# Retention state kept as 64 x 64 blocks instead of zero-padded 128 x 128 blocks, with heads m and m + 4 paired

## The chip, the cores and the metric

One core of one Trainium2 chip runs the whole program. The metric is the device time of one execution in microseconds (us), median of several runs.

## The reference

Three stages follow one another. Stage one is retention (attention with a decay and no softmax) for 4 sequences, 8 heads, 576 positions, 64 wide:

```python
scores = scale * np.matmul(q, k.transpose(0, 1, 3, 2))
gamma = 1.0 - 2.0 ** (-5.0 - np.arange(H))
Dmat = np.where(rel >= 0, gamma[:, None, None] ** rel, 0.0)    # rel = i - j
x = np.matmul(scores * Dmat, v)                                # -> 2304 tokens x 512
```

Stage two sends every token to one of 8 experts (argmax of x @ w_gate), runs relu(x @ w1) @ w2 there and multiplies by the gate. Stage three is a dense layer with a softmax-weighted activation and a layer norm. The change is in stage one.

## The kernel before, in words

**Retention by chunks.** Each of the 4 sequences is cut into 4 chunks of 128 positions and a last one of 64, so there are 20 chunks; c is a chunk's place in its sequence (0 to 4). For a chunk, the output x is the sum of two products. The *value products* (L437) multiply the decayed scores P inside the chunk with v. The *state products* (L432, only for c > 0) multiply the decayed queries qd with the state S that earlier chunks of the sequence left. After the chunk, S is updated: 8 products kd x v go to PSUM (o_D, L446) and VectorE adds them to S (o_Sadd, L456 and L458); the last chunk of a sequence needs no update.

**Tiles of the TensorE array.** All of this is float32, and each float32 matmul leaves two records (two passes) in the trace. The page writes the part of the array that a matmul uses as rows*columns: 128*64 is half the columns, 64*128 half the rows, 64*64 a quarter. Two heads share the 128 partitions of qT, kT and qd. In S the two heads of a pair stand on the diagonal of a 128 x 128 block, and the rest of the block is zeros that are set once. So a state product contracts over all 128 rows, gives both heads of a pair at once (128 columns out), and uses 128*64: 64 positions at a time, 8 matmuls for a full chunk. Value products use 128*64 as well, 16 matmuls of 64 columns. The scores (o_S, L417) use row halves, one head of a pair on each.

**The order of work.** The order on every engine is written by hand. PERIOD lists the steps of one period; ('PV', 2) means that period i runs the step for chunk i - 2. DRAIN writes out what follows period 19. Around the change it reads, in a period: T (transposes of k and q, age 0), S (age 1), D (age 2), Sq (age 3, ScalarE: sum of squares of x; bs on VectorE and pw, a power on GpSimd, make a factor of it), ..., R and L (routing, ages 6 and 5), PV (age 2), X (age 4, transposes of normalised rows), hi (age 3, ScalarE: x times its factor to half precision), Sadd (age 2), xr (age 4, ScalarE), lo (age 3, VectorE: the rest of x). So Sq, hi and lo read x of chunk i - 3 in the period in which PV writes x of chunk i - 2. x has two buffers, each one PSUM bank (psX, bufs=2). In DRAIN, hi:17 stands behind PV:18, hi:18 ahead of PV:19, and lo:18 behind PV:19.

**Loads.** SyncE issues every load in one in-order queue (load, L354). Each k and each v of a chunk is one DMA (L368), each q of two chunks one DMA (L365). Loads of chunk i + 3 are issued in period i, once their buffers are free (k has 4, v 6, q 4).

**What comes behind.** DRAIN scatters the routed rows to memory, loads the first 192 rows of expert 0 back (L540) and runs them (ehm, L256 to L258). The experts and stage three follow, each in one fixed order.

Of the kernel before, what the change touches and what calls it, by code (L numbers as in the profile page):

```python
# [10 lines left out]
F32 = mybir.dt.float32  # L11
# [10 lines left out]
DM = H * D  # L22
E = 8
F = 1024
CH = 128
# [30 lines left out]
def host_constants():  # L56

    gam = 1.0 - 2.0 ** (-5.0 - np.arange(H, dtype=np.float64))
    p = np.arange(128)
    slot = 2 * (np.arange(H) % 4) + np.arange(H) // 4  # L60
    i_j = (p[None, :] - p[:, None])[:, None, :].astype(np.float64)
    decay = np.where(i_j >= 0, gam[slot][None, :, None] ** np.maximum(i_j, 0.0), 0.0) * (XS / np.sqrt(float(D)))
    pair = gam[2 * np.arange(4)[None, :] + (p // 64)[:, None]]
    qdec = pair[:, :, None] ** (CH + p)[None, None, :].astype(np.float64) * (XS / np.sqrt(float(D)))
    kdec = gam[None, None, :] ** -(np.arange(CPB)[None, :, None] * CH + p[:, None, None]).astype(np.float64)
    f = {}
    f["ident"] = np.eye(128)
    f["gch"] = pair ** float(CH)
    f["kdec"] = kdec.reshape(128, -1)
    f["iota8"] = np.tile(np.arange(E), (128, 1))  # L70
    f["ebase"] = np.tile(np.arange(E) * NR, (128, 1))
    f["tri8"] = np.tile((np.arange(E)[None, :] < np.arange(E)[:, None]).astype(np.float32).reshape(1, -1), (128, 1))
    f["cols"] = np.tile([COLS[0] - EARLY] + list(COLS[1:]), (128, 1))
    f["first"] = np.tile([100.0 * E * NR] + [float(E - e) for e in range(1, E)], (128, 1))
    f["nrows"] = np.tile([rows16(c) for c in COLS], (128, 1))

    un = p[:, None] + 128 * np.arange(NUT)[None, :]
    f["unit"] = np.concatenate([un % NUNIT, p[:, None] % (UNIT - 1)], axis=1)
    f["uexp"] = 1 + np.concatenate([un // NUNIT, p[:, None] // (UNIT - 1)], axis=1)
    f["iblk"] = np.tile(np.arange(NBLK), (128, 1))  # L80
    f["nhalf"] = np.tile([-0.5, 0.5], (128, 1))
    cols, parts, at = {}, [], 0
    for k, a in f.items():
        cols[k] = (at, at + a.shape[1])
        at += a.shape[1]
        parts.append(a.astype(np.float32))
    c32 = np.ascontiguousarray(np.concatenate(parts, axis=1), dtype=np.float32)
    h = {}
    h["ident16"] = np.eye(128)
    h["tris"] = (p[:, None] < p[None, :]).astype(np.float32)  # L90
    h["ones"] = np.ones((128, 128))
    h["iota128"] = np.tile(p, (128, 1))

    h["ida"], h["idb"] = np.zeros((128, NCH)), np.zeros((128, NCH))
    for ch in range(NCH):
        b, c = divmod(ch, CPB)
        n = min(CH, S - c * CH)
        h["ida"][:n, ch], h["idb"][:n, ch] = np.divmod(b * S + c * CH + np.arange(n) - NOID, 64)
    h["ida"] *= 64
    h["acc0"] = np.tile(np.arange(E) * (NR // 128), (128, 1))  # L100
    cols16, parts, at = {}, [], 0
    for k, a in h.items():
        cols16[k] = (at, at + a.shape[1])
        at += a.shape[1]
        parts.append(a.astype(np.float16))
    c16 = np.ascontiguousarray(np.concatenate(parts, axis=1), dtype=np.float16)
    tok = np.zeros((1, 1), dtype=np.int32)
    return (c32, cols, c16, cols16, tok, np.ascontiguousarray(decay.reshape(128, -1), dtype=np.float32),
            np.ascontiguousarray(qdec, dtype=np.float32))
# [3 lines left out]
def tile_attention_moe_solu(ctx: ExitStack, tc: tile.TileContext, a: dict, cols, cols16):  # L113
# [216 lines left out]


    at_stack = ExitStack()
    psX = at_stack.enter_context(tc.tile_pool(name="psX", bufs=2, space=PSUM))
    ap_ = at_stack.enter_context(tc.tile_pool(name="attn", bufs=2))
    at_one = at_stack.enter_context(tc.tile_pool(name="at_one", bufs=1))
    st = [dict() for _ in range(NCH + 1)]
    decay = at_one.tile([128, H, 128], F32, name="decay")
    qdec = at_one.tile([128, CPB - 1, 4, 128], F32, name="qdec")

    states = [at_one.tile([128, 4, 128], F32, name=f"S{i}") for i in range(2)]  # L340
    misc = psB.tile([128, 512], F32, tag="b1", name="misc")
    sps = misc[:, 0:4 * D].rearrange("p (m d) -> p m d", d=D)
    lgp = misc[:, 4 * D:4 * D + 2 * E].rearrange("p (t e) -> p t e", e=E)
# [7 lines left out]
    def heads(t, n):  # L351
        return t[:n].rearrange("p (h d) -> p h d", h=H)

    def load(ch, names="qkv"):  # L354

        b, c = divmod(ch, CPB)
        n = csize(ch)
        for nm in names:
            if nm == "q":
                if c % 2:  # L360
                    st[ch]["q"] = st[ch - 1]["q"]
                    continue
                n2 = min(2 * CH, S - c * CH)
                t = ap_.tile([128, H, 2, D], F32, tag="q", bufs=4, name="q")
                sp.dma_start(t[:n2 // 2], a["q"][b, :, c * CH:c * CH + n2, :].rearrange("h (p r) d -> p h r d", r=2))  # L365
            else:
                t = ap_.tile([128, DM], F32, tag=nm, bufs={"k": 4, "v": 6}[nm], name=nm)
                sp.dma_start(heads(t, n), a[nm][b, :, c * CH:c * CH + n, :].rearrange("h p d -> p h d"))  # L368
            st[ch][nm] = t

    def o_T(ch, n, s):
# [14 lines left out]
    def q_half(ch, n, s, o):  # L386

        for r in range(2):
            yield (s["qT"][64 * o:64 * o + 64, :, :n].rearrange("p m (j r) -> p m r j", r=2)[:, :, r],
                   s["qp"][64 * r:64 * r + 64, o::2, :n // 2])  # L390

    def o_qe(ch, n, s):
        s["qT"] = ap_.tile([128, 4, 128], F32, tag="qT", name="qT")
# [29 lines left out]

    def o_PV(ch, n, s):
        b, c = divmod(ch, CPB)
        xo = s["x"] = psX.tile([128, DM], F32, tag="b0", name="xo")

        halves = [slice(i, i + 64) for i in range(0, n, 64)]
        if c:
            for m in range(4):  # L430
                for i in halves:
                    pe.matmul(xo[i, m * 128:(m + 1) * 128], lhsT=s["qd"][:, m, i], rhs=states[b % 2][:, m, :],  # L432
                              start=(m == 0), stop=False)
        for h in range(H):
            d = slice(h * D, (h + 1) * D)
            for i in halves:
                pe.matmul(xo[i, d], lhsT=s["P"][:n, 4 * (h % 2) + h // 2, i], rhs=s["v"][:n, d],  # L437
                          start=(c == 0 and h == 0), stop=(h == H - 1))

    def o_D(ch, n, s):  # L440
        if ch % CPB == CPB - 1:
            return
        for m in range(4):
            for r in range(2):
                h = 2 * m + r
                pe.matmul(sps[64 * r:64 * r + 64, m, :], lhsT=s["kd"][:n, h * D:(h + 1) * D], rhs=s["v"][:n, h * D:(h + 1) * D],  # L446
                          start=(m == 0), stop=(m == 3))

    def o_Sadd(ch, n, s):
        b, c = divmod(ch, CPB)  # L450
        if c == CPB - 1:
            return
        for r in range(2):
            d = states[b % 2][64 * r:64 * r + 64, :, 64 * r:64 * r + 64]
            if c == 0:
                dve.tensor_copy(d, sps[64 * r:64 * r + 64])  # L456
            else:
                dve.tensor_tensor(d, d, sps[64 * r:64 * r + 64], op=ALU.add)  # L458

    def o_Sq(ch, n, s):  # L460
        junk = ap_.tile([128, DM], F16, tag="junk", name="junk")
        s["ss"] = ap_.tile([128, 1], F32, tag="ss", name="ss")
        act.activation(junk[:n], s["x"][:n], AF.Square, accum_out=s["ss"][:n])

    def o_bs(ch, n, s):
        s["base"] = ap_.tile([128, 1], F32, tag="base", name="base")
# [4 lines left out]

    def o_hi(ch, n, s):
        s["row"] = ap_.tile([128, 2 * DM], F16, tag="row", bufs=9, name="row")
        act.activation(s["row"][:n, 0:DM], s["x"][:n], AF.Copy, scale=pwall[:n, ch, 0:1])

    def o_lo(ch, n, s):
        dve.scalar_tensor_tensor(s["row"][:n, DM:2 * DM], s["x"][:n], pwall[:n, ch, 0:1], s["row"][:n, 0:DM],
                                 op0=ALU.mult, op1=ALU.subtract)

    def o_X(ch, n, s):  # L480
# [153 lines left out]
    def warm(n):  # L634

        if n:
            ps = psX.tile([128, DM], F32, tag="b0", name="wps")
            for _ in range(n):
                pe.matmul(ps, lhsT=zero[:, 0:128], rhs=zero[:, 0:DM], start=True, stop=True)

    def setup():
        dve.memset(zero, 0.0)
        warm(WARM[0])
        sp.dma_start(c32, a["c32"])
        load(0, "k")
        load(0, "q")
        load(1, "kq")
        sp.dma_start(decay, a["decay"].rearrange("p (h i) -> p h i", h=H))
        sp.dma_start(qdec[:, 0], a["qdec"])
        load(0, "v")  # L650
        load(2, "kq")
        load(1, "v")
        sp.dma_start(c16, a["c16"])
        load(2, "v")
        for t in states:
            pool.memset(t, 0.0)
        pool.memset(idxall, 0.0)
        pool.memset(slotall, 2.0 * BIG)
        pool.memset(sloti, int(2 * BIG))
        pool.memset(lgall, 0.0)  # L660
        pool.memset(pwall, 1.0)
# [572 lines left out]
```

## Time and profile before

| | |
|---|---|
| median of 3 runs | 530.83 us (529.23 to 533.39) |
| profiled execution | 529.27 us, of which the span is 527.4 us |
| mean granted TensorE clock | 0.994 of 2.4 GHz |
| TensorE matmul busy | 504.9 us, 96% of the span |
| VectorE, ScalarE, GpSimd busy | 348.3, 278.9, 150.8 us |
| retention periods that follow one another without a load to wait for | 31 to 105 us |

The profile's page shares out busy time by engine and by groups of instructions; the trace behind it gives every instruction's start, duration and what ended the idle time before it. A time such as "59.48" is us from the start of the span. Matmuls overlap, so the distance from the start of one group of matmuls to the start of the next is what counts, not the busy time of a group.

### The profile page before, as it was taken

The numbers are of one execution on the slowest core, as the hardware profiler recorded it, in microseconds if no ns is written. First come the engines' busy times: TensorE is split into PE (matmuls) and PEld (weight loads), VectorE is DVE, ScalarE is ACT, GpSimd is POOL, SyncE is SP. The second block draws the span as 40 slices with busy tenths as digits, with TensorE's granted clock in tenths as the row PEclk, the third lists the DMA queues.
The fourth block names the chain that finished last, engine by engine and source line by source line (L and its number), as shares of the span: only waits on it lengthen the run. The fifth ranks groups of instructions, "written<-read, shape, count | busy, mean of one in ns | idle before, by whom it ended". The sixth has DMA issues, their size and how long they took to land.

```text
span 527.4 us, 11770 instructions
## 1 busy us (share of the span) xinstructions
PE 504.9 (96%) x4616; PEld 341.2 (65%) x4616; DVE 348.3 (66%) x839; ACT 278.9 (53%) x452; POOL 150.8 (29%) x183
## 2 busy tenths in 40 slices
PE   8889999999998999999999998999999999999992
PEld 4779999989975677777777786444444444444440
DVE  0478778878657796969889994386565555556520
ACT  4688888873445646465657661264434433443430
POOL 3638687844650000202010000022221231131130
PEclk9999999999999999999999999999999999999997
DMA  8999998222689796968798830037234333333431
GB/s 214 228 248 247 256 284 208 103 62 91 177 265 281 239 257 225 250 212 253 259 238 274 219 121 0 1 64 116 60 81 93 68 80 82 79 76 71 94 81 44
DMA packets 139485, 83.09 MB, mean 158 GB/s; under 512 B 100053, under 2 KB 126581, under 8 KB 139389
## 3 DMA queue, kind: packets, MB, share of 16 engines
q1 hardware_dynamic: 135742, 72.53, 54.5%
q0 software_dynamic: 3680, 9.74, 5.3%
q8 instruction: 38, 0.62, 0.5%
q14 instruction: 25, 0.20, 0.2%
HBM read 57.21 MB, written 15.21 MB: 137 GB/s over the span
## 4 chain that ended last, share of the span: by engine, by line
PE 69%; DMA 10%; DVE 9%; issue 4%; ACT 2%; SPq 2%; POOL 1%; POOLq 0%; DVEq 0%; ACTq 0%
PE hp L1049 6%; PE hp L1048 6%; PE hp L1047 6%; PE op L1087 5%; PE op L1088 5%; PE op L1089 5%; PE yps L282 4%; PE yps L280 4%; PE yps L281 4%; DMA wst<-in_w 4%; PE hps L256 3%; PE hps L258 3%; PE hps L257 3%; PE sc L417 3%; PE xo L437 3%
## 5 line engine op out<-in xcount | busy, mean ns | idle before, releaser
L178 ACT ACTIVATE wh<-wst 128x1024 f16<-128x1024 f32 x64 | 67.1, 1054 | 45.5 <-DMA wst<-in_w 45.1
L181 DVE SCALAR_TENSOR_TENSOR wl<-wst,wh 128x1024 f16<-128x1024 f32 x64 | 77.7, 1231 | 2.9 <-ACT wh L178 1.4
L282 PE MATMUL yps<-hl,wh 128*128 128x144 f16 (+7 forms) x256 | 72.0, 286 | 2.5 <-DVE hl L266 2.5
L256 PE MATMUL hps<-xT,wh 128*128 128x144 f16 (+7 forms) x256 | 72.0, 286 | 2.3 <-DVE hl L266 2.1
L280 PE MATMUL yps<-hh,wh 128*128 128x144 f16 (+7 forms) x256 | 72.0, 286 | 0.5 <-DVE hl L266 0.5
L281 PE MATMUL yps<-hh,wl 128*128 128x144 f16 (+7 forms) x256 | 72.0, 286 | 0.0
L258 PE MATMUL hps<-xT,wl 128*128 128x144 f16 (+7 forms) x256 | 72.0, 286 | 0.0
L257 PE MATMUL hps<-xT,wh 128*128 128x144 f16 (+7 forms) x256 | 72.0, 286 | 0.0
L1062 POOL TENSOR_TENSOR t<-t,c 128x2 f32<-128x2 f32 x18 | 12.7, 705 | 185.4 <-DVE t L1061 185.4
L1087 PE MATMUL op<-w_out_hi,uT 128*128 128x512 f16 x144 | 54.6, 379 | 0.0
L1047 PE MATMUL hp<-w_in_hi,y_hi 128*128 128x512 f16 x144 | 54.6, 379 | 0.0
L1048 PE MATMUL hp<-w_in_lo,y_hi 128*128 128x512 f16 x144 | 54.6, 379 | 0.0
L1088 PE MATMUL op<-w_out_lo,uT 128*128 128x512 f16 x144 | 54.6, 379 | 0.0
L1089 PE MATMUL op<-w_out_hi,uT 128*128 128x512 f16 x144 | 54.6, 379 | 0.0
L1049 PE MATMUL hp<-w_in_hi,y_lo 128*128 128x512 f16 x144 | 54.4, 379 | 0.0
L1055 ACT ACTIVATE ex<-hp,t,ct 128x1024 f32<-128x1024 f32 x18 | 21.7, 1205 | 50.6 <-DVE t L1053 50.6
L870 POOL TENSOR_TENSOR sc<-sc,vals 128x180 bf16<-128x180 bf16 x10 | 8.7, 867 | 104.3 <-DVE sc L838 59.3
L422 DVE TENSOR_TENSOR P<-sc,decay 128x1024 f32<-128x1024 f32 (+1 forms) x20 | 22.3, 1114 | 22.0 <-PE sc L417 22.0
L1057 DVE SCALAR_TENSOR_TENSOR u<-hp,ex 128x1024 f32<-128x1024 f32 x18 | 22.0, 1223 | 21.7 <-ACT ex L1055 21.7
L1060 ACT ACTIVATE jk<-u,t 128x1024 f16<-128x1024 f32 x18 | 20.7, 1148 | 27.9 <-DVE t L1058 21.3
L280 PEld LDWEIGHTS <-wh 128*128 128x128 f16 x288 | 28.2, 98 | 10.4 <-issue 3.1
L257 PEld LDWEIGHTS <-wh 128*128 128x128 f16 x288 | 28.2, 98 | 9.9 <-issue 2.7
(223 smaller groups left out, 1069.2 us busy)
## 6 DMA issues: line engine op xcount, KB each, us to landing
wst<-in_w SPq DMA_DIRECT2D x64, 512.0 KB, 4.9
k<-in_k SPq DMA_DIRECT2D x16, 256.0 KB, 6.0
q<-in_q SPq DMA_DIRECT2D x8, 512.0 KB, 7.1
v<-in_v SPq DMA_DIRECT2D x16, 256.0 KB, 5.8
f64raw<-in_w_in SPq DMA_DIRECT2D x8, 512.0 KB, 4.1
f64raw<-in_w_out SPq DMA_DIRECT2D x8, 512.0 KB, 4.8
xs<-zero SPq DMA_DIRECT2D x1, 672.0 KB
decay<-in_decay SPq DMA_DIRECT2D x1, 512.0 KB, 7.2
```

Source lines behind the costliest of these rows:

```text
L256: pe.matmul(ps[:, i, :n], lhsT=hi[:, c0:c0 + 128], rhs=x[:, kk, :n], start=(kk == 0), stop=False)
L257: pe.matmul(ps[:, i, :n], lhsT=hi[:, c0:c0 + 128], rhs=x[:, 4 + kk, :n], start=False, stop=False)
L258: pe.matmul(ps[:, i, :n], lhsT=lo[:, c0:c0 + 128], rhs=x[:, kk, :n], start=False, stop=(kk == 3))
L280: pe.matmul(ps[:, i, :n], lhsT=hi[:, c0:c0 + 128], rhs=hh[:, kk, :n], start=(kk == 0), stop=False)
L281: pe.matmul(ps[:, i, :n], lhsT=lo[:, c0:c0 + 128], rhs=hh[:, kk, :n], start=False, stop=False)
L282: pe.matmul(ps[:, i, :n], lhsT=hi[:, c0:c0 + 128], rhs=hl[:, kk, :n], start=False, stop=(kk == 7))
L1047: pe.matmul(hp[:, i], lhsT=yh[:, kk], rhs=w_in_hi[:, kk, c], start=(kk == 0), stop=False)
L1048: pe.matmul(hp[:, i], lhsT=yh[:, kk], rhs=w_in_lo[:, kk, c], start=False, stop=False)
L1049: pe.matmul(hp[:, i], lhsT=yl[:, kk], rhs=w_in_hi[:, kk, c], start=False, stop=(kk == 3))
L1087: pe.matmul(op, lhsT=s["uT"][:, kk], rhs=w_out_hi[:, kk], start=(kk == 0), stop=False)
L1088: pe.matmul(op, lhsT=s["uT"][:, kk], rhs=w_out_lo[:, kk], start=False, stop=False)
L1089: pe.matmul(op, lhsT=s["uT"][:, 8 + kk], rhs=w_out_hi[:, kk], start=False, stop=(kk == 7))
```

## The change

The state becomes 64 x 64 per head: S is 128 partitions x 4 x 64, head m in the lower and head m + 4 in the upper 64 partitions, without zeros. For c = 1, 2, 3 a state product takes one head and 64 positions: it uses a quarter of the array (64*64), and a chunk has 16 such products of 64 columns instead of 8 of 128. The lower and the upper row half write to different PSUM banks: x of heads 0 to 3 lies in one bank and x of heads 4 to 7 in another, and one tile (xall) of two banks holds x of two chunks, each chunk in one half of both banks. For the last chunk of a sequence (c = 4, 64 positions) the state is put into a second array with zeros (whole), and its products contract over 128 rows as before, now 8 of 64 columns instead of 4 of 128.

VectorE's update is one instruction of 128 partitions for c = 0, 1, 2 and two of 64 for c = 3. Pairs of heads change from (2m, 2m + 1) to (m, m + 4); so that k has them side by side, each k is loaded with two DMAs, one for heads 0 to 3 and one for 4 to 7. Sq, hi and lo read x as two runs of 256. Constants follow the order of the heads.

```diff
-    psX = at_stack.enter_context(tc.tile_pool(name="psX", bufs=2, space=PSUM))
+    psX = at_stack.enter_context(tc.tile_pool(name="psX", bufs=1, space=PSUM))
...
-    states = [at_one.tile([128, 4, 128], F32, name=f"S{i}") for i in range(2)]
+    states = [at_one.tile([128, 4, D], F32, name=f"S{i}") for i in range(2)]
+    whole = [at_one.tile([128, 2, 4, D], F32, name=f"W{i}") for i in range(2)]
+    xall = psX.tile([128, 2, 2, DM // 2], F32, name="xall")
...
-                sp.dma_start(heads(t, n), a[nm][b, :, c * CH:c * CH + n, :].rearrange("h p d -> p h d"))
+                src = a[nm][b, :, c * CH:c * CH + n, :]
+                if nm == "k":
+                    for r in range(2):
+                        sp.dma_start(t[:n].rearrange("p (m r d) -> p m r d", m=4, r=2)[:, :, r], src[4 * r:4 * r + 4].rearrange("m p d -> p m d"))
+                else:
+                    sp.dma_start(heads(t, n), src.rearrange("h p d -> p h d"))
...
-        xo = s["x"] = psX.tile([128, DM], F32, tag="b0", name="xo")
+        xo = s["x"] = xall[:, :, ch % 2]
         if c:
             for m in range(4):
+                for r in range(2):
+                    for i in halves:
+                        if c == CPB - 1:
+                            lhsT, rhs = s["qd"][:, m, i], whole[b % 2][:, r, m, :]
+                        else:
+                            lhsT, rhs = s["qd"][64 * r:64 * r + 64, m, i], states[b % 2][64 * r:64 * r + 64, m, :]
+                        pe.matmul(xo[i, r, m * D:(m + 1) * D], lhsT=lhsT, rhs=rhs, start=(m == 0), stop=False)
+        for m in range(4):
+            for r in range(2):
+                h = 4 * r + m
                 for i in halves:
-                    pe.matmul(xo[i, m * 128:(m + 1) * 128], lhsT=s["qd"][:, m, i], rhs=states[b % 2][:, m, :],
-                              start=(m == 0), stop=False)
...
+                    pe.matmul(xo[i, r, m * D:(m + 1) * D], lhsT=s["P"][:n, h, i], rhs=s["v"][:n, h * D:(h + 1) * D],
+                              start=(c == 0 and m == 0), stop=(m == 3))
...
+        d = states[b % 2]
+        if c == 0:
+            dve.tensor_copy(d, sps)
+        elif c == CPB - 2:
+            for r in range(2):
+                o = slice(64 * r, 64 * r + 64)
+                dve.tensor_tensor(whole[b % 2][o, r], d[o], sps[o], op=ALU.add)
+        else:
+            dve.tensor_tensor(d, d, sps, op=ALU.add)
```

## Rows read from the trace of the kernel before

**Rows 1.** Windows: per stretch, busy us (count) of each engine, clock, DMA share, GB/s.

```profile
23.00:24.00 1.00, 0.72 (x26) 0.58 (x21) 0.68 (x2) 0.92 (x1) 0.95 (x1) 1.00 0.31 41
...
31.00:105.00 74.00, 73.96 (x1412) 67.19 (x1414) 57.10 (x195) 62.43 (x137) 55.87 (x66) 1.00 0.92 224
...
117.00:127.00 10.00, 9.58 (x128) 9.01 (x128) 8.22 (x38) 4.05 (x7) 6.64 (x8) 1.00 0.21 81
```

**Rows 2.** Timeline, first loads: start, duration, engine, line, what; in brackets idle and releaser.

```profile
23.59 0.75 SPq L368 DMA_DIRECT2D k<-in_k  x1
...
31.04 0.63 PE L376 MATMUL tp<-c,k 128*128 128x128 f32 x4 [1.59 <-DMA k<-in_k]
```

**Rows 3.** Timeline of TensorE over most of one period (state and value products of chunk 8).

```profile
57.72 0.68 PE L417 MATMUL sc<-qT,kT 64*64 64x64 f32 x16
58.33 0.69 PE L446 MATMUL misc<-v,kd 128*64 128x64 f32 x16
58.95 0.19 PE L498 MATMUL misc<-oh,c 64*64 64x8 f16 x1
59.07 0.19 PE L499 MATMUL misc<-acc,c 128*64 128x8 f16 x1
...
59.48 1.09 PE L432 MATMUL xo<-S,qd 128*64 128x128 f32 x16
60.40 1.10 PE L437 MATMUL xo<-v,P 128*64 128x64 f32 x32
61.44 0.62 PE L483 MATMUL xp<-c,row 128*128 128x128 f16 x8
```

**Rows 4.** Timeline of TensorE, windows of 0.03 and 0.08 us.

```profile
59.48 0.33 PE L432 MATMUL xo<-S,qd 128*64 128x128 f32 x2
...
60.40 0.28 PE L437 MATMUL xo<-v,P 128*64 128x64 f32 x4
```

**Rows 5.** Timeline of TensorE: products of chunk 4 (c = 4), then of chunk 5 (c = 0).

```profile
38.62 1.09 PE L432 MATMUL xo<-S,qd 128*64 128x128 f32 x8
39.64 1.14 PE L437 MATMUL xo<-v,P 64*64 64x64 f32 x16
40.72 0.62 PE L483 MATMUL xp<-c,row 128*128 128x128 f16 x8
...
44.25 1.15 PE L437 MATMUL xo<-v,P 128*64 128x64 f32 x32
45.33 0.62 PE L483 MATMUL xp<-c,row 128*128 128x128 f16 x8
```

**Rows 6.** Timeline of ScalarE: kT of chunk 2 read from its transposes.

```profile
15.88 0.60 ACT L384 ACTIVATE kT<-tp 128x512 f32<-128x512 f32 x1 [2.69 <-PE tp L380]
```

**Rows 7.** Timeline of ScalarE in the period of rows 3: xr.

```profile
62.15 1.02 ACT L487 ACTIVATE xr<-xp 128x1024 f16<-128x1024 f16 x1 [0.53 <-PE xp L483]
```

**Rows 8.** Timeline of ScalarE in the drain: hi of 17, Sq of 18, hi of 18.

```profile
110.96 0.68 ACT L474 ACTIVATE row<-xo,pwall 128x512 f16<-128x512 f32 x1
112.12 0.60 ACT L463 ACTIVATE junk<-xo 128x512 f16<-128x512 f32 x1 [0.48 <-PE xo L437]
...
113.80 0.69 ACT L474 ACTIVATE row<-xo,pwall 128x512 f16<-128x512 f32 x1
```

**Rows 9.** Timeline of VectorE in the drain: lo of 17, Sadd of 18, lo of 18.

```profile
111.67 0.75 DVE L477 SCALAR_TENSOR_TENSOR row<-xo,pwall,row 128x512 f16<-128x512 f32 x1
...
112.94 0.85 DVE L458 TENSOR_TENSOR S<-S,misc 64x256 f32<-64x256 f32 x2
...
115.13 0.75 DVE L477 SCALAR_TENSOR_TENSOR row<-xo,pwall,row 128x512 f16<-128x512 f32 x1
```

**Rows 10.** Timeline of TensorE in the drain: state products of 19, X of 18, first expert.

```profile
113.85 1.09 PE L432 MATMUL xo<-S,qd 128*64 128x128 f32 x8 [0.48 <-DVE S L458]
...
116.21 0.61 PE L483 MATMUL xp<-c,row 128*128 128x128 f16 x8
117.08 0.24 PE L256 MATMUL hps<-ex,wh 128*128 128x192 f16 x1 [0.27 <-DMA ex<-xs]
```

More of the change, by code (lines that the diff above doesn't have):

```diff
@@ L59, in host_constants @@
     p = np.arange(128)
-    slot = 2 * (np.arange(H) % 4) + np.arange(H) // 4
     i_j = (p[None, :] - p[:, None])[:, None, :].astype(np.float64)
-    decay = np.where(i_j >= 0, gam[slot][None, :, None] ** np.maximum(i_j, 0.0), 0.0) * (XS / np.sqrt(float(D)))
-    pair = gam[2 * np.arange(4)[None, :] + (p // 64)[:, None]]
+    decay = np.where(i_j >= 0, gam[None, :, None] ** np.maximum(i_j, 0.0), 0.0) * (XS / np.sqrt(float(D)))
+    pair = gam[np.arange(4)[None, :] + 4 * (p // 64)[:, None]]
     qdec = pair[:, :, None] ** (CH + p)[None, None, :].astype(np.float64) * (XS / np.sqrt(float(D)))
-    kdec = gam[None, None, :] ** -(np.arange(CPB)[None, :, None] * CH + p[:, None, None]).astype(np.float64)
+    kdec = gam[np.arange(H).reshape(2, 4).T.reshape(-1)][None, None, :] ** -(np.arange(CPB)[None, :, None] * CH + p[:, None, None]).astype(np.float64)
     f = {}
@@ L389, in q_half @@
             yield (s["qT"][64 * o:64 * o + 64, :, :n].rearrange("p m (j r) -> p m r j", r=2)[:, :, r],
-                   s["qp"][64 * r:64 * r + 64, o::2, :n // 2])
+                   s["qp"][64 * r:64 * r + 64, 4 * o:4 * o + 4, :n // 2])
     def o_qe(ch, n, s):
@@ L430, in o_PV @@
             for m in range(4):
-                for i in halves:
-                    pe.matmul(xo[i, m * 128:(m + 1) * 128], lhsT=s["qd"][:, m, i], rhs=states[b % 2][:, m, :],
-                              start=(m == 0), stop=False)
[L434 to L438, printed above, removed]
+                for r in range(2):
[8 more added lines that the diff above has]
+                h = 4 * r + m
+                for i in halves:
+                    pe.matmul(xo[i, r, m * D:(m + 1) * D], lhsT=s["P"][:n, h, i], rhs=s["v"][:n, h * D:(h + 1) * D],
+                              start=(c == 0 and m == 0), stop=(m == 3))
     def o_D(ch, n, s):
@@ L444, in o_D @@
             for r in range(2):
-                h = 2 * m + r
-                pe.matmul(sps[64 * r:64 * r + 64, m, :], lhsT=s["kd"][:n, h * D:(h + 1) * D], rhs=s["v"][:n, h * D:(h + 1) * D],
+                h, kc = 4 * r + m, (2 * m + r) * D
+                pe.matmul(sps[64 * r:64 * r + 64, m, :], lhsT=s["kd"][:n, kc:kc + D], rhs=s["v"][:n, h * D:(h + 1) * D],
                           start=(m == 0), stop=(m == 3))
@@ L452, in o_Sadd, with halved @@
             return
[L453 to L458, printed above, removed]
+        d = states[b % 2]
[7 more added lines that the diff above has]
+            dve.tensor_tensor(d, d, sps, op=ALU.add)
+    def halved(t, n):
+        return t.rearrange("p (r w) -> p r w", r=2)[:n]
     def o_Sq(ch, n, s):
@@ L462, in o_Sq @@
         s["ss"] = ap_.tile([128, 1], F32, tag="ss", name="ss")
-        act.activation(junk[:n], s["x"][:n], AF.Square, accum_out=s["ss"][:n])
+        act.activation(halved(junk[:], n), s["x"][:n], AF.Square, accum_out=s["ss"][:n])
     def o_bs(ch, n, s):
@@ L473, in o_hi @@
         s["row"] = ap_.tile([128, 2 * DM], F16, tag="row", bufs=9, name="row")
-        act.activation(s["row"][:n, 0:DM], s["x"][:n], AF.Copy, scale=pwall[:n, ch, 0:1])
+        act.activation(halved(s["row"][:, 0:DM], n), s["x"][:n], AF.Copy, scale=pwall[:n, ch, 0:1])
     def o_lo(ch, n, s):
-        dve.scalar_tensor_tensor(s["row"][:n, DM:2 * DM], s["x"][:n], pwall[:n, ch, 0:1], s["row"][:n, 0:DM],
+        dve.scalar_tensor_tensor(halved(s["row"][:, DM:2 * DM], n), s["x"][:n], pwall[:n, ch, 0:1], halved(s["row"][:, 0:DM], n),
                                  op0=ALU.mult, op1=ALU.subtract)
@@ L636, in warm @@
         if n:
-            ps = psX.tile([128, DM], F32, tag="b0", name="wps")
             for _ in range(n):
-                pe.matmul(ps, lhsT=zero[:, 0:128], rhs=zero[:, 0:DM], start=True, stop=True)
+                pe.matmul(xall[:, 0].rearrange("p t w -> p (t w)"), lhsT=zero[:, 0:128], rhs=zero[:, 0:DM], start=True, stop=True)
     def setup():
@@ L654, in setup @@
         load(2, "v")
-        for t in states:
+        for t in whole:
             pool.memset(t, 0.0)
```

## The prediction

> **What bounds the kernel now.** I read the table of windows first, to find the stage that the change touches and what is full there. From 31 to 105 us, sixteen periods of retention, TensorE is busy 73.96 of 74.00 us; ScalarE follows with 62.43, VectorE with 57.10 [rows 1]. Busy is not the same as fast, since matmuls overlap, so I read next where this time goes: the timeline of one period, group start to group start [rows 3]. There is no wait in it, and the only idle time of TensorE in the whole stretch lies at its very beginning, at 31.04, where the transposes of chunk 5 wait for the load of its k [rows 2]. Until then the loads set the pace, after that TensorE's own instructions. Behind the periods, the drain is a chain in which TensorE, ScalarE and VectorE hand each other the last chunks [rows 8 to 10], and from 117 to 127 us TensorE is full again with the first expert [rows 1]. So a period's gain on TensorE reaches the end unless a load or the drain takes it back, and the reader should price three things: the products, the loads ahead of 31 us, and the drain.
>
> **State and value products, c = 1 to 3.** Now 16 records of 128 columns on two column halves take 0.92 us (59.48 to 60.40), and the 32 records of the value products behind them 1.04 us (60.40 to 61.44), together 1.96 us [rows 3]. The change makes 32 records of 64 columns on four quarters. No row shows four quarters at work together. What rows show is two tiles together: two records start within one window of 0.03 us and four within 0.08 us [rows 4], on column halves; and 16 records of 64 columns take 0.61 us on two row halves (57.72 to 58.33) and 0.62 us on two column halves (58.33 to 58.95), the change of tile shape behind them included [rows 3]. Bounds for the new group: four quarters keep the pace per tile of two halves, so 32 records take what 16 take on two, 0.62 us; or no more than two tiles ever run together, and it takes what 32 records on two halves take, 1.08 us (44.25 to 45.33, a chunk without state products) [rows 5]; or, the far end, one at a time as in the last chunk, 1.08 us for 16 records [rows 5], so 2.1 us. I take 0.62: row halves and column halves overlap equally well, each by itself, and nothing in the rows ties them to one another.
>
> A second cost comes with it: the tile shape now changes between state and value products, 64*64 to 128*64. Two routing matmuls of 8 columns and different shapes start 0.12 us apart (58.95, 59.07) [rows 3]; so a change costs about 0.1 us. It is in the 0.62, and the value products then begin after a change, as in a chunk without state: 1.08 instead of 1.04 us. Sum 0.62 + 1.08 = 1.70, against 1.96: **-0.26 us a chunk**. Ten of the twelve such chunks run their products after 31 us (chunk 3, and three in each later sequence), so -2.6 us; the two before it only lengthen TensorE's wait for the load.
>
> A rule of the Trainium skill speaks against this. TensorE: Matmul & The Clock Gate, section "Wait — 56ns, not 53.3ns?", says that start-to-start never falls below about 25 ns however small the matmul is. The rows differ for matmuls on different tiles: two starts in 0.03 us, four in 0.08 us [rows 4]. By the rule 32 records would need at least 0.80 us, an estimate from that page, in place of the roughly 0.5 us inside the 0.62, and the gain of a chunk would be gone.
>
> **The last chunk, c = 4.** 8 records of 128 columns on one tile take 1.02 us (38.62 to 39.64); 16 of 64 columns on one tile take 1.08 (39.64 to 40.72) [rows 5]. So +0.06 four times, **+0.24 us**.
>
> **The update of the state.** One VectorE instruction less in three chunks of each sequence, about 0.42 us each (half of the 0.85 of a pair) [rows 9]. VectorE is not the bound in the periods [rows 1], and the drain's own update, chunk 18 with c = 3, keeps two instructions. I take nothing; at most 0.4 us could come back where a drain step stands behind the update of chunk 17.
>
> **x in one tile of two banks.** Sq, hi and lo keep their elements, as two runs of 256; nothing. But two chunks' x now share a tile. Row 15.88 shows how such a tile is guarded: kT is read from the first bank of a transposes' tile, whose k half had been written before, yet ScalarE waited 2.69 us until the q transposes, in the other bank, were done [rows 6]. So I expect hi of chunk i - 3 to wait for PV of chunk i - 2, which stands ahead of it in program order. In a period this is covered: behind hi on ScalarE stands xr, which waits until X, itself behind PV on TensorE, is done (0.53 us idle ahead of 62.15) [rows 7], and hi at 0.69 us [rows 8] fits almost wholly between the ends of PV and X, whose group takes about 0.6. Less than 0.1 us moves on to Sq, ke, qe and qf, and ScalarE has 11.6 of 74 us free [rows 1]. If this cover were gone, TensorE would lose up to the 0.26 of each chunk again.
>
> In the drain there is no cover. hi:17 (110.96) now waits for PV:18, whose end let Sq:18 start at 112.12 [rows 8]. So hi:17 runs from 112.12 and pushes Sq:18 by about 0.65; lo:17 on VectorE (111.67, 0.75 us) moves behind hi:17, and Sadd:18, ended at 113.79, by the same 0.65 [rows 9]; the power on GpSimd and hi:18 (113.80) follow, so hi:18 ends near 115.1 [rows 8]. PV:19 started at 113.85 when Sadd:18 was done [rows 10]; now it waits for hi:18 as well, near 115.15, +1.3. Queued behind it on TensorE are X:18 and the first expert. lo:18 (115.13) [rows 9] now waits for the end of PV:19, near 117.3, and ends at 118.1; X:18 (116.21) needs it and runs at 118.15, and the first expert's matmuls come at 118.6 instead of 117.08 [rows 10]: **+1.5 us**. What was late there before, the load of ex, has 0.27 us of its wait in it already. Lower bound 0, if regions are guarded more finely than the row shows; upper bound 2.3, if a read on ScalarE also waits for VectorE's read of the same bank (Sq:18 behind lo:17, another 0.75). I take 1.5, the row's own way. TensorE is full afterwards [rows 1], so nothing takes it back.
>
> **k in two DMAs.** 20 more issues on SyncE, of the same bytes in the same pieces. After 31 us no load is waited for. Before it one matters: chunk 5's k, issued at 23.59 in 0.75 us and awaited at 31.04 [rows 2]. Just ahead, from 23 to 24 us, the DMA engines stood at a share of 0.31 and 41 GB/s [rows 1]: there SyncE's pace, not bandwidth, set the flow, and the second issue for chunk 4's k lies right in front of it. Between 0 (the queue catches up behind it) and two issues of 0.6 to 0.75 (1.2 to 1.5); I take **+0.5 us**. Earlier and later issues are hidden behind full DMA engines, or behind loads that nobody waits for.
>
> **Sum.** -2.6 + 0.24 + 1.5 + 0.5 = -0.36 us on a profiled execution of 529.27 us (span 527.4), so 528.9; carried to the median of 530.83, 1.6 above it, **530.4 us**. Under about 1% (5.3 us) a measurement of this kernel can't be told from no change.
>
> **The rivals.** First, *no more than two tiles together*. Each chunk then pays 1.08 + 1.08 = 2.16 against 1.96, +0.20; ten times +2.0; with 0.24, 1.5 and 0.5 it is +4.2: 535.1, slower than before. It decides where the mean spacing of the 32 records passes 23 ns: 1.96 - 1.08 leaves 0.88 for the group, less some 0.15 for its end and the change of shape. For it: no row with four tiles, and the 34 ns a record of the two-tile group with all 32 [rows 5]. Against it: starts 0.03 us apart or less across tiles [rows 4]. The skill's floor of 25 ns, above, would end on this side of the point too. Chance 0.2. Second, *the drain is not held up*, since the two halves of xall are told apart: -2.6 + 0.24 + 0.5 = -1.9, 528.9. Against it stands [rows 6], one row in which the releaser is inferred. Chance 0.2. Third, *quarters don't overlap at all* when they add to an open sum: 2.1 + 1.08 = 3.2 a chunk, +1.2 ten times, with the rest +14: 545. The equal overlap on row and column halves speaks against it. Chance 0.04. Fourth, *loads become the bound*: the DMA share is 0.92 from 31 to 105 us already [rows 1], and a shorter period asks for more; then the gain of the periods is lost and 533.1 is left (530.83 + 0.24 + 1.5 + 0.5). Against it: no load was waited for in 74 us. Chance 0.08. The forecast as summed keeps 0.48.
>
> **How the numbers follow.** The likeliest case's own range, from the bounds of the drain and the loads, is 528.5 to 532. Down to the second rival, with the spread of the runs (529.23 to 533.39 for one kernel), gives a low end of 527; up to the first rival a high end of 535. Faster by over 1% needs 525.5 or less: no case reaches it, 0.04 for what I don't see. Slower by over 1% needs 536.1: the third rival and the upper part of the first, 0.09. The rest, 0.87, is within 1%.
>
> **What would show it.** In the new timeline: L432's successor as a group of 32 records of 64*64 starting 0.6 us ahead of the value products (1.1 in the first rival, 2.1 in the third); the value products of c > 0 at 1.08 us; transposes of chunk 5 near 31.5; hi released by the value products of the next chunk; in the drain PV:19 waiting for ScalarE's hi:18, and the first expert about 1.5 us later behind chunk 18's products than now. The prediction is wrong if four quarters run slower than two halves, if hi's wait reaches TensorE in every period, or if the drain keeps its old order.

## The result and the profile after

The changed kernel takes **535.28 us** (median of 11 runs, 533.66 to 537.54), the kernel before 529.87 us beside it (11 runs, 527.63 to 533.39). The ratio is 1.0100 with a 95% interval of 1.0074 to 1.0125: slower by 1%, just past the high end of the forecast range. The profiled execution took 537.16 us (span 535.4), against 529.27 (span 527.4) before. TensorE's mean granted clock is 0.981, against 0.994.

I read the periods first. The timeline of the changed kernel, TensorE, chunks with c = 3 and c = 4 (start, duration, engine, line, what):

```profile
59.23 0.69 PE L446 MATMUL xall<-S,qd 64*64 64x64 f32 x32
59.85 1.15 PE L451 MATMUL xall<-v,P 128*64 128x64 f32 x32
60.94 0.23 PE L503 MATMUL xp<-c,row 128*128 128x128 f16 x1
...
63.85 1.15 PE L446 MATMUL xall<-W,qd 128*64 128x64 f32 x16
64.93 1.14 PE L451 MATMUL xall<-v,P 64*64 64x64 f32 x16
```

From start to start the quarters take 0.62 us and the value products 1.09, where the group before took 0.92 and 1.04 [rows 3]. So the products came out within 0.01 us of the forecast. The last chunk's state products take 1.08 us, as forecast, against 1.02 [rows 5].

The loss lies behind the periods. Chunk 19's transposes start at 102.15 us, 0.37 earlier than before (102.52). The first matmul of the first expert starts at 121.40, and before it started at 117.08 [rows 10]. The drain of the changed kernel on the timeline (in brackets the idle time ahead and what ended it):

```profile
102.15 0.44 PE L385 MATMUL tp<-c,k 64*128 64x64 f32 x4
...
112.49 0.69 ACT L494 ACTIVATE row<-xall,pwall 128x512 f16<-128x512 f32 x1 [1.11 <-PE xall L451]
...
113.08 0.59 ACT L483 ACTIVATE junk<-xall 128x512 f16<-128x512 f32 x1
...
113.86 0.75 DVE L497 SCALAR_TENSOR_TENSOR row<-xall,pwall,row 128x512 f16<-128x512 f32 x1 [1.87 <-ACT junk L483]
...
114.58 0.86 DVE L473 TENSOR_TENSOR W<-S,misc 64x256 f32<-64x256 f32 x2
114.67 0.40 PE L503 MATMUL xp<-c,row 128*128 128x128 f16 x4 [1.03 <-DVE base L487]
...
115.47 0.69 ACT L494 ACTIVATE row<-xall,pwall 128x512 f16<-128x512 f32 x1 [0.77 <-POOL pwall L490]
...
116.21 1.97 PE L446 MATMUL xall<-W,qd 128*64 128x64 f32 x16 [1.15 <-ACT row L494]
...
118.11 1.97 PE L451 MATMUL xall<-v,P 64*64 64x64 f32 x16
...
120.19 0.75 DVE L497 SCALAR_TENSOR_TENSOR row<-xall,pwall,row 128x512 f16<-128x512 f32 x1 [3.34 <-PE xall L451]
...
120.30 1.30 PE L503 MATMUL xp<-c,row 128*128 128x128 f16 x8
...
121.40 0.37 PE L255 MATMUL hps<-ex,wh 128*128 128x192 f16 x1
```

Two things are to be seen. First the waits: hi:17 (112.49) waits for PV:18; Sq:18 (113.08) comes behind it; lo:17 on VectorE (113.86) waits until Sq:18 on ScalarE has read x; Sadd:18 and the power follow; hi:18 (115.47) follows the power; PV:19 (116.21) waits for hi:18, and lo:18 (120.19) for PV:19. Before, PV:19 started at 113.85 [rows 10] and lo:18 at 115.13 [rows 9]. Second the durations: the two groups of PV:19 take 1.90 and 1.90 us from start to start, and before 1.02 and 1.07 [rows 10]. The windows of the same stretch (TensorE's busy time stands first behind the length of the window, the granted clock third from the end) show the clock beside them:

```profile
111.00:113.00 2.00, 2.00 (x62) 1.81 (x57) 0.84 (x6) 0.89 (x2) 0.85 (x2) 1.00 0.33 74
113.00:116.00 3.00, 1.03 (x18) 0.59 (x14) 2.01 (x8) 2.23 (x5) 0.85 (x2) 0.94 0.57 130
116.00:125.00 9.00, 8.68 (x73) 8.01 (x74) 2.96 (x19) 2.44 (x5) 2.80 (x4) 0.50 0.07 28
```

TensorE was busy for 1.03 of the 3 us from 113 to 116; near the end of them, at 115.7, its granted clock fell to 0.50, the 1.2 GHz level, and it came back at 125.9. PV:19, X:18 and a part of the first expert run in this stretch. Before, the clock was 1.00 from 105 to 118 us.

### The profile page after: what moved, and what is told of

Same layout as the page of the kernel before. It is cut to its first block, busy times and chain, and to the rows that moved or that the text cites. A ratio compares the mean times of both kernels' runs of the same rounds, so it can differ in the third digit from the quotient of the medians.

```text
span 535.4 us, 12261 instructions
## 1 busy us (share of the span) xinstructions
PE 510.0 (95%) x4840; PEld 344.1 (64%) x4840; DVE 342.3 (64%) x827; ACT 278.9 (52%) x452; POOL 152.9 (29%) x183
## 4 chain that ended last, share of the span: by engine, by line
PE 71%; DVE 9%; DMA 5%; issue 5%; SPq 3%; POOL 2%; ACT 2%; POOLq 0%; DVEq 0%; ACTq 0%
PE hp L1068 6%; PE hp L1067 6%; PE hp L1066 6%; DMA wst<-in_w 5%; PE op L1106 5%; PE op L1107 5%; PE op L1108 5%; PE yps L281 4%; PE yps L279 4%; PE yps L280 4%; PE hps L255 4%; PE hps L257 4%; PE hps L256 4%; PE xall L451 4%; PE sc L426 3%
## 5 line engine op out<-in xcount | busy, mean ns | idle before, releaser
L255 PE MATMUL hps<-xT,wh 128*128 128x144 f16 (+7 forms) x256 | 72.0, 286 | 2.2 <-DVE hl L265 2.2
L256 PE MATMUL hps<-xT,wh 128*128 128x144 f16 (+7 forms) x256 | 72.0, 286 | 0.0
L256 PEld LDWEIGHTS <-wh 128*128 128x128 f16 x288 | 28.7, 99 | 9.7 <-issue 2.5
L280 PEld LDWEIGHTS <-wl 128*128 128x128 f16 x288 | 28.2, 98 | 9.3 <-issue 2.0
```

The source lines that it names most:

```text
L255: pe.matmul(ps[:, i, :n], lhsT=hi[:, c0:c0 + 128], rhs=x[:, kk, :n], start=(kk == 0), stop=False)
L256: pe.matmul(ps[:, i, :n], lhsT=hi[:, c0:c0 + 128], rhs=x[:, 4 + kk, :n], start=False, stop=False)
L280: pe.matmul(ps[:, i, :n], lhsT=lo[:, c0:c0 + 128], rhs=hh[:, kk, :n], start=False, stop=False)
```

## The experiments

**The theory:** the shared tile makes reads and writes of different chunks wait for one another in the drain; TensorE idles; its clock falls; the waits and the clock together take back more than the quarters gain. **The rivals:** the quarters, or the greater number of matmuls (4840 records in the changed kernel, 4616 before), lose time in small gaps that the profile after shows inside TensorE's streams, some 1.4 us in all; or the two DMAs of k cost what is missing. Ratios below are the recorded ones to the kernel before on the same chip, with 95% intervals; they are not quotients of the medians shown. The kernel before had a median of 529.87 us beside the changed kernel, 530.63 beside the next four kernels of the table and 530.90 beside the last three.

| kernel | median us | ratio | first expert's matmuls behind the transposes of chunk 19 | its y products |
|---|---|---|---|---|
| before (profile) | 529.87 | | 14.56 us | 24.45 us |
| changed (profile) | 535.28 | 1.0100 (1.0074 to 1.0125) | 19.25 | 31.29 |
| before, shared tile | 538.74 | 1.0178 (1.0146 to 1.0211) | 18.59 | 30.75 |
| x of chunk 18 apart | 528.72 | 0.9972 (0.9950 to 0.9994) | 13.84 | 23.73 |
| idle time filled | 532.87 | 1.0064 (1.0040 to 1.0088) | 17.04 | 26.94 |
| no quarters | 534.64 | 1.0090 (1.0057 to 1.0124) | 17.64 | 29.50 |
| x of chunk 18 apart, no quarters | 531.14 | 1.0008 (0.9982 to 1.0034) | 14.26 | 24.14 |
| before, k halved | 530.38 | 0.9998 (0.9966 to 1.0029) | 14.14 | 24.02 |
| changed, again | 534.36 | 1.0065 (1.0038 to 1.0093) | 17.03 | 28.97 |

The last two columns are differences of two starts in each profile: first matmul of the first expert (L255 or L256), and first of its y products (the second product of an expert, yps), less the start of chunk 19's transposes.

### The shared tile alone, in the kernel before

```diff
-    psX = at_stack.enter_context(tc.tile_pool(name="psX", bufs=2, space=PSUM))
+    psX = at_stack.enter_context(tc.tile_pool(name="psX", bufs=1, space=PSUM))
+    xall = psX.tile([128, 2, 2, DM // 2], F32, name="xall")
...
-        xo = s["x"] = psX.tile([128, DM], F32, tag="b0", name="xo")
+        xo = s["x"] = xall[:, :, ch % 2]
...
+                    pe.matmul(xo[i, m // 2, (m % 2) * 128:(m % 2 + 1) * 128], lhsT=s["qd"][:, m, i], rhs=states[b % 2][:, m, :],
+                              start=(m % 2 == 0), stop=False)
...
```

The value products write to the same two halves, and Sq, hi and lo read x as two runs of 256.

> The kernel before, with one edit: x in one tile of two banks, each chunk in one half of both (heads 0 to 3 in one bank, 4 to 7 in the other), read as two runs of 256. No quarters, no other pairs, k in one DMA. If the shared tile is the cause: the drain shows the waits of the changed kernel (hi:17 behind the products of chunk 18, lo:17 and Sq:18 one behind the other, products of chunk 19 behind hi:18), the granted clock falls behind 115 us, and the time is 6 to 8 above the kernel before, 536 to 538, worse than the changed kernel by the gain of the quarters. If the shared tile is innocent: within 1 of the kernel before.

Measured: 538.74 us, 1.8% above the kernel before by the ratio, and 0.7 above the range that I gave. The drain of this kernel on the timeline:

```profile
111.72 0.59 ACT L467 ACTIVATE junk<-xall 128x512 f16<-128x512 f32 x1
...
112.50 0.75 DVE L481 SCALAR_TENSOR_TENSOR row<-xall,pwall,row 128x512 f16<-128x512 f32 x1 [1.88 <-ACT junk L467]
...
114.11 0.69 ACT L478 ACTIVATE row<-xall,pwall 128x512 f16<-128x512 f32 x1 [0.77 <-POOL pwall L474]
...
114.85 1.97 PE L433 MATMUL xall<-S,qd 128*64 128x128 f32 x8 [1.15 <-ACT row L478]
...
120.03 0.37 PE L256 MATMUL hps<-ex,wh 128*128 128x192 f16 x1
```

The same waits, to 0.02 us, and the same half clock (0.50 from 114.5 to 124.7 us), with the old products, pairs and loads. The periods are untouched: from chunk 5's transposes to chunk 19's it takes 71.45 us, before 71.48. So the loss of this execution is the tile's and comes in the drain. The profiled execution (535.64 us) is the fastest of the six, and no trace shows where the slower ones lose more. That the changed kernel stays below this one agrees with a gain of its quarters, but two medians this far apart don't size it.

### x of chunk 18 in a tile of its own

```diff
-        xo = s["x"] = xall[:, :, ch % 2]
+        if ch == NCH - 2:
+            xo = s["x"] = psA.tile([128, 2, 512], F32, tag="A", name="x18")[:, :, 0:DM // 2]
+        else:
+            xo = s["x"] = xall[:, :, ch % 2]
```

> The changed kernel, but x of chunk 18 alone lies in a two-bank tile of its own (the one that the scores of chunk 18 have left) instead of in xall. Theory (the shared tile holds up the drain, TensorE idles, its clock falls to 1.2 GHz): hi:17 no longer waits for the products of chunk 18, nor those of chunk 19 for hi:18, nor lo:18 for those of chunk 19; the granted clock stays 1.00 from 115 to 126 us, the products of chunk 19 take about 1.1 and 1.1 us in place of 1.97 and 1.97, the first expert starts near 117 and the time is 527.5 to 530, that is 5 to 8 below the changed kernel and 0 to 2 below the kernel before. Rival (what was lost lies in the quarters, in the gaps inside TensorE's streams, or in the two DMAs of k): the time stays within 2 of the changed kernel's, 533 to 537.

Measured: 528.72 us, inside the theory's range, and by the ratio 0.28% (0.06 to 0.50) below the kernel before. Its drain on the timeline, and two windows:

```profile
101.65 0.43 PE L385 MATMUL tp<-c,k 64*128 64x64 f32 x4
...
109.05 0.69 PE L449 MATMUL x<-S,qd 64*64 64x64 f32 x32
...
110.39 0.69 ACT L497 ACTIVATE row<-xall,pwall 128x512 f16<-128x512 f32 x1 [0.33 <-POOL pwall L493]
...
110.98 0.59 ACT L486 ACTIVATE junk<-x 128x512 f16<-128x512 f32 x1
111.11 0.75 DVE L500 SCALAR_TENSOR_TENSOR row<-xall,pwall,row 128x512 f16<-128x512 f32 x1 [0.45 <-ACT row L497]
...
112.30 1.49 PE L449 MATMUL xall<-W,qd 128*64 128x64 f32 x16
...
112.73 0.69 ACT L497 ACTIVATE row<-x,pwall 128x512 f16<-128x512 f32 x1
...
113.71 1.14 PE L454 MATMUL xall<-v,P 64*64 64x64 f32 x16
...
115.49 0.25 PE L255 MATMUL hps<-ex,wh 128*128 128x192 f16 x1
...
125.38 0.24 PE L279 MATMUL yps<-ehh,wh 128*128 128x192 f16 x1
```

```profile
115.00:117.00 2.00, 2.00 (x35) 2.00 (x32) 1.22 (x10) 1.02 (x3) 1.19 (x3) 1.00 0.00 0
117.00:126.00 9.00, 8.66 (x119) 8.10 (x117) 7.76 (x34) 3.60 (x7) 5.23 (x7) 1.00 0.29 107
```

hi:17 no longer waits for TensorE, lo:17 runs beside Sq:18 (111.11 and 110.98), and PV:19 starts ahead of hi:18. The clock stays at 1.00. The rivals, under which this kernel would have stayed near 535, are out: it has the quarters, the matmuls and the two DMAs of k.

### TensorE's idle time filled, the waits left in

The order of the drain, cut down to the edit (`...` stands for steps that stay):

```diff
-            ... Sq:17 X:16 ... wa ch:16 X:17 sd:15 hi:18 PV:19 ...
+            ... Sq:17 w:5 X:16 ... wa ch:16 w:4 X:17 sd:15 hi:18 w:5 PV:19 ...
```

Each w step is that many matmuls of zeros into a tile that nobody reads.

> The changed kernel, with 14 matmuls of zeros (half precision, 512 columns, 0.21 us each) on TensorE in the drain: 5 ahead of X:16, 4 ahead of X:17 and 5 ahead of the products of chunk 19, into a tile that nobody reads. They fill idle time and take no wait away. If the fall of the clock is the larger part of the loss: the waits stay (first expert near 118.5 to 119.5 instead of 121.4, against 117.1 before), the granted clock stays 1.00, the products of chunk 19 take 1.1 us each, and the time comes 3 to 5 below the changed kernel, 530 to 532. If the waits alone are the loss: no gain, 535 or up to 1 more.

Measured: 532.87 us, 2.4 below the changed kernel's first measurement. Its drain on the timeline:

```profile
100.97 0.44 PE L385 MATMUL tp<-c,k 64*128 64x64 f32 x4
...
109.06 0.69 PE L446 MATMUL xall<-S,qd 64*64 64x64 f32 x32
...
111.52 1.02 PE L662 MATMUL wps<-zero 128*128 128x512 f16 x4
...
112.30 0.75 DVE L497 SCALAR_TENSOR_TENSOR row<-xall,pwall,row 128x512 f16<-128x512 f32 x1 [2.03 <-ACT junk L483]
...
113.34 1.24 PE L662 MATMUL wps<-zero 128*128 128x512 f16 x5
...
114.65 1.15 PE L446 MATMUL xall<-W,qd 128*64 128x64 f32 x16
...
115.72 1.14 PE L451 MATMUL xall<-v,P 64*64 64x64 f32 x16
...
118.01 0.25 PE L255 MATMUL hps<-ex,wh 128*128 128x192 f16 x1
...
127.91 0.24 PE L279 MATMUL yps<-ehh,wh 128*128 128x192 f16 x1
```

lo:17 still waits for Sq:18, but the products of chunk 19 take 1.07 and 1.08 us, and the granted clock is 1.00 from 107 to 127 us. In the drain, then, work that computes nothing gained time, since it kept the clock: the y products come 2.0 to 4.4 us earlier than in the two profiles of the changed kernel. Over the whole kernel that gain isn't shown. The ratio of 1.0064 is below the changed kernel's first one, 1.0100, but the same as its second, 1.0065; and in this profile a later wait for a load (2.4 us, from 148.4 us on) let the clock fall again, from 151.7 to 155.1 us.

This run also parts the loss in two, by the last column of the table, against the kernel with x of chunk 18 apart, which has neither part. This profile stands 26.94 - 23.73 = 3.2 us behind it; 0.7 of that are the five matmuls ahead of X:16, since the products of chunk 18 start 8.09 us behind chunk 19's transposes (109.06 - 100.97) and there 7.40 (109.05 - 101.65). So **the waits alone cost 2.5 us**. The changed kernel stands 7.6 us behind, and in its second profile 5.2. In the first of these two, 1.1 us is idle time that the profile puts down to no wait (hi:16 starts 0.8 us later behind chunk 19's transposes than in the second, and 0.2 lies inside PV:18). So **the clock cost 4.0 us there and 2.7 in the second**. The median of this run is 0.9 above the range that I gave for the clock and 2 below the one for the waits alone, so the rows of the drain decide between the two, not the median.

### No quarters

```diff
-                        if c == CPB - 1:
-                            lhsT, rhs = s["qd"][:, m, i], whole[b % 2][:, r, m, :]
-                        else:
-                            lhsT, rhs = s["qd"][64 * r:64 * r + 64, m, i], states[b % 2][64 * r:64 * r + 64, m, :]
+                        lhsT, rhs = s["qd"][:, m, i], whole[b % 2][:, r, m, :]
...
```

The rest of the edit keeps the state in whole alone, so VectorE's update is two instructions of 64 partitions for every c, as in the kernel before.

> The changed kernel, but all state products contract over 128 rows of a state with zeros (128*64, 64 columns, two tiles together) as in the last chunk of a sequence; the same number of matmuls, the same shared tile, pairs and DMAs. The group of 32 records takes 1.08 us instead of 0.62 and the value products 1.04 instead of 1.09: +0.41 in ten chunks behind 31 us, +4.1: 539 to 540. If the small gaps inside TensorE's streams (about 0.2 us each, six of them) come from the number of instructions, they are here too; if they come from the quarters, they are gone and the time is 1 to 1.5 less.

Measured: 534.64 us, where I expected 539 to 540. Two things were wrong in that. The group takes 0.98 us and not 1.08, as the timeline of this kernel shows:

```profile
59.46 1.15 PE L441 MATMUL xall<-W,qd 128*64 128x64 f32 x32
60.44 1.10 PE L446 MATMUL xall<-v,P 128*64 128x64 f32 x32
```

No change of tile shape stands between the two groups, so a chunk loses 0.3 us, not 0.41; from chunk 5's transposes to chunk 19's it takes 72.14 us, against 69.83 in the kernel with x of chunk 18 apart. And this kernel's clock fell later (117.8 instead of 115.7 us), so that chunk 19's state products still ran in 1.08 us. Over its six runs the mean clock went from 0.984 to 0.995 and the time from 537.72 to 532.12. With the drain in that condition the worth of the quarters can't be read from this kernel. So I ran the same edit on the kernel that keeps its clock:

> x of chunk 18 in a tile of its own, and no quarters (state products over 128 rows with zeros, 64 columns, as many matmuls): the quarters by themselves, without the drain's loss. The profiles of the runs with and without quarters give 0.98 us instead of 0.62 for the group of 32 records and 5.34, 5.54, 5.41 instead of 5.03, 5.33, 5.10 us for the periods: 0.3 in each of 10 chunks, so 2.5 to 3.5 above the kernel with x of chunk 18 apart, 531 to 532.5, and at or just above the kernel before. If the quarters' gain is lost elsewhere: within 1 of it, 528 to 529.7.

Measured: 531.14 us. The median lies inside the range, and without the quarters the kernel is where it was before (ratio 1.0008). The two kernels ran beside different runs of the kernel before, 0.24 us above one median and 1.91 below the other, so **the quarters are worth about 2 us**: 2.2 by these differences, 1.9 by the two ratios, 2.4 by the bare medians, a little under the 2.5 to 3.5 that I expected. The intervals of the two ratios overlap slightly; what makes the gain sure is the timelines, 0.2 to 0.3 us in every period with quarters.

### k in two DMAs, in the kernel before

```diff
-                sp.dma_start(heads(t, n), a[nm][b, :, c * CH:c * CH + n, :].rearrange("h p d -> p h d"))
+                src = a[nm][b, :, c * CH:c * CH + n, :]
+                if nm == "k":
+                    for r in range(2):
+                        sp.dma_start(heads(t, n)[:, 4 * r:4 * r + 4], src[4 * r:4 * r + 4].rearrange("h p d -> p h d"))
+                else:
+                    sp.dma_start(heads(t, n), src.rearrange("h p d -> p h d"))
```

> The kernel before with one edit: each k by two DMAs of four heads. By the prediction's term the transposes of chunk 5 start 0.5 us later than before (31.5), the time 0.5 more (bounds 0 and 1.5). If SyncE catches up: 31.0 and no difference.

Measured: 530.38 us against 530.90, no difference. Its halves of k lie side by side where the changed kernel lays them in turns. Chunk 5's transposes in this kernel:

```profile
30.11 0.41 PE L381 MATMUL tp<-c,k 128*128 128x128 f32 x2 [0.70 <-DMA k<-in_k]
```

They start 0.9 us earlier than in the profile of before [rows 2]. Over all nine profiles this start lies between 29.99 and 31.82 us, with one DMA and with two, so the spread of one execution is larger than the term that I priced at 0.5.

### The changed kernel once more, and the gaps

The first profile after has gaps inside TensorE's streams for which no wait is shown, such as this one in the scores of chunk 13 ("issue" is idle time for which the profile shows no releaser):

```profile
77.07 0.71 PE L426 MATMUL sc<-qT,kT 64*128 64x128 f32 x6
78.04 0.38 PE L426 MATMUL sc<-qT,kT 64*128 64x128 f32 x3 [0.26 <-issue]
```

> The changed kernel once more, unedited, beside the two others on this chip. The single gaps inside TensorE's streams of its first profile (0.2 to 0.5 us at 44.6, 77.5, 100.3 and 111.1) were in none of the four kernels with the same or nearly the same stream: they belong to that execution, so they are gone or elsewhere; transposes of chunk 19 about 70 us behind those of chunk 5 in place of 71.1. The drain's waits and the fall of the clock are there again, time 534 to 537. If the gaps come from the quarters with the shared tile: the same places again.

Measured: 534.36 us. The old places are clean, but a new one stands in the state products of chunk 7, and the clock fell near the start, in the drain and once more from 165.5 to 168.9 us:

```profile
34.84 1.10 PE L446 MATMUL xall<-S,qd 64*64 64x64 f32 x32
...
55.27 0.34 PE L446 MATMUL xall<-S,qd 64*64 64x64 f32 x8
55.87 0.52 PE L446 MATMUL xall<-S,qd 64*64 64x64 f32 x20 [0.25 <-issue]
...
116.20 1.15 PE L446 MATMUL xall<-W,qd 128*64 128x64 f32 x16 [1.15 <-ACT row L494]
117.28 1.64 PE L451 MATMUL xall<-v,P 64*64 64x64 f32 x16
...
120.24 0.37 PE L255 MATMUL hps<-ex,wh 128*128 128x192 f16 x1
```

From chunk 5's transposes to chunk 19's it takes 71.98 us, not the 70 expected: 0.5 us in the gap, and most of the rest, 1.3, where the clock stood at 0.50 from 32.4 to 35.8 us (the quarters at 34.84 take 1.03 us from start to start instead of 0.62). The waits of the drain are there again, and so is the half clock, from 117.7 us on, in the middle of PV:19's value products (117.28). Such gaps also came in the kernel without quarters and with x of chunk 18 apart (the period from 77.21 us lasts 5.92 us, the same one of the sequence before 5.58), while the kernel before, the shared tile alone, the x of chunk 18 apart and the filled idle time have none. So they go with single executions and aren't tied to the quarters; what makes them stays open.

## Why the prediction was wrong

**Products: right.** 0.62 and 1.09 us against the forecast 0.62 and 1.08, and 1.08 in the last chunk. The first rival (no more than two tiles together, 535.1 us) gave nearly the measured time by a mechanism that isn't there; the third is out as well. By the floor of 25 ns of the Trainium skill (TensorE: Matmul & The Clock Gate, section "Wait — 56ns, not 53.3ns?"), taken as one that holds across tiles, 32 records would have needed 0.80 us. The trace disagrees: the 32 records start within 0.47 us. One reading was loose: the 16 records that the prediction calls row halves are marked 64*64 [rows 3], quarters, of which two on different row halves were at work; the bound of 0.62 us doesn't hang on it. The gain over the periods is a little smaller than forecast: from chunk 5's transposes to chunk 19's 71.48 - 69.83 = 1.65 us, where eight times 0.26 less three times 0.06 make 1.90. One period in three gains 0.15 instead of 0.25 (5.48 to 5.33): there the state products before already began beside the last routing matmuls, without a change of shape between them.

**Loads, the update of the state: right to within what can be seen.** The two DMAs of k cost nothing measurable (forecast 0.5, bounds 0 and 1.5); chunk 5's transposes start at 31.08 us in the changed kernel, at 31.04 before, and the forecast was 31.5. The rival of the loads (533.1) is out as well: between the transposes of chunk 6 and those of chunk 19 TensorE waits for no load in any of the nine profiles.

**The drain: the step that failed.** It said "+1.5 us", "upper bound 2.3", and took the case in which a read on ScalarE doesn't wait for VectorE's read. The waits came link by link as written (hi:17 behind PV:18, PV:19 behind hi:18, lo:18 behind PV:19), but the term was too small by two things. The smaller: reads do wait for reads, here VectorE's for ScalarE's, the other way round from the case behind the upper bound. lo:17 waited until Sq:18 was done, in every profile in which both lie in xall (1.63 to 2.03 us of idle time ahead of it), and ran beside it where x of chunk 18 lies elsewhere. The waits cost 2.5 us, 2.3 of it up to the start of PV:19 (12.99 us behind chunk 19's transposes in the second profile of the changed kernel, 10.65 with x of chunk 18 apart). The Trainium skill has the rule that I should have weighed in place of that one row: PSUM — Partial Sum Buffer, section "PSUM bank collisions raise a hardware error", says that two engines may not touch the same bank on the same partitions at once, whichever columns, and reads against reads included. Here two chunks share both banks. The trace agrees (lo:17 starts at 113.86, when Sq:18, begun at 113.08, has read), though no run here tells whether the order is kept by the bank or by the tile.

The larger: the prediction saw TensorE wait and priced the wait, and didn't ask what the wait does to its clock. So the clock's term stood at nothing without a reason, and it cost 2.7 to 4.0 us more. With both measured terms the sum is -1.9 (528.72 - 530.63, everything but the drain's loss), +2.5 and +2.7 to 4.0: +3.3 to +4.6 on the kernel before. The two measurements of the changed kernel say +3.5 (534.36 - 530.90) and +5.4 (535.28 - 529.87). The rest of the higher one is of the size of the gaps that only single executions show, but no run assigns it to them. The clock's part differs from one execution to the next: in both measurements the fastest run is the one with the highest mean granted clock (533.66 us at 0.993, 531.96 us at 0.994; the others 0.979 to 0.991).

**The second rival** (drain not held up, 528.9) has been built: with x of chunk 18 apart the profiled execution took 528.15 us and the median is 528.72. That is 1.9 us below the kernel before, just what the prediction's other terms add up to, and the drain alone made the forecast wrong. That the two agree to a tenth is luck in part: the interval of this run is 0.3 to 2.7 us below, the 0.5 for k shows in no run, and the periods gained 0.25 less than forecast.

## What to carry to other kernels

When two buffers are merged into one tile or one bank, list every engine that reads or writes either of them, reads too, and walk the place where the pipeline runs empty: in the full periods there was cover for each new wait, in the drain none. Where TensorE gets a new wait of a microsecond or two, price the clock of the work behind it as well: here it cost as much as the wait and more. A buffer that is only needed in the drain can come from a pool that is running empty there; one such tile turned +1% into -0.3%.

## What was not expected of the hardware

- Four quarters of the array each keep the pace that two tiles have: 32 float32 records of 64 columns take the 0.62 us that 16 take on two tiles. They start within about 0.47 us, the four of a round 7 ns apart and the rounds 58 ns apart. At the 1.2 GHz level the whole group takes 1.03 us instead of 0.62.
- TensorE's clock fell to its 1.2 GHz level in or behind the second of two waits of 1.0 and 1.15 us that came close together, at 115.7 us in the changed kernel (117.7 in its second profile), 114.5 with the shared tile alone and 117.8 without quarters, and was back between 124.5 and 126. The same waits filled with matmuls of zeros left it at 1.00.
- The same idle stretch doesn't always end alike: ahead of chunk 5's transposes TensorE idles for 1.6 us in the kernel before and 1.7 in the second run of the changed one (about 29.5 to 31 us); in the first the clock stayed at 1.00, in the second it stood at 0.50 from 32.4 to 35.8 and cost about 1.3 us. In four other profiles it had fallen earlier, between 25 and 28 us, and was back at 31.2 us at the latest.
